# Float64 weights to float32 by an integer sum on POOL, one softmax form for all batches, one-sum pooling, and a reordered beginning

## The chip, the cores and the metric

One core of one Trainium2 chip runs the whole program. The metric is the device time of one launch in microseconds (us); the kernel before takes 567.24 us, the median of 3 runs (565.05 to 570.59). Engines: PE is TensorE, DVE VectorE, ACT ScalarE, POOL GpSimd, SP the engine that issues most DMAs.

## The reference

Attention over keys and values pooled by 8, then a mixing block:

```python
B, H, S, D = 8, 8, 576, 64;  Sp = 72;  d_model = H * D = 512
k_p = k.reshape(B, H, Sp, 8, D).mean(axis=3)
v_p = v.reshape(B, H, Sp, 8, D).mean(axis=3)
scores = scale * np.matmul(q, k_p.transpose(0, 1, 3, 2))
attn = softmax(scores)                       # sum + 1e-9 below the line
x = np.matmul(attn, v_p)                     # -> (B, S, 512)
theta = x @ w_theta
zr, zi = x * np.cos(theta), x * np.sin(theta)
y = einsum('ts,bsd->btd', w_tok_r, zr) + einsum('ts,bsd->btd', w_tok_i, zi)
u = x + y
return u + np.maximum(u @ w_ch, 0.0)
```

`q`, `k`, `v` are float32. The four weights (`w_theta` and `w_ch` 512 x 512, `w_tok_r` and `w_tok_i` 576 x 576) arrive as float64, and the kernel reads them as pairs of 32-bit words.

## The kernel before, in words

Work is cut into small generators ("streams"), and a long table of words, `SCHEDULE`, says which generator takes its next step; a last letter v, g or a gives that step's free choice of engine to DVE, POOL or ACT. So the table sets the order of instructions on every engine, and each engine works in that order. The word before the dot names the kind and batch: `k`, `v`, `Q` load (Q also transposes), `K` and `V` pool, `S` is a softmax tile of 128 queries, `X` attention times V, `T` the rotation by theta, `Z` and `M` split and mix over tokens, `F` the last channel matmul. `h` is a 128-row piece of `w_theta`, `c` one of `w_ch`, `w` a piece of the token weights, `W` its transposes into `WTh` and `WTl`. `D` is a warm-up of 12 matmuls.

A float64 becomes float32 in `to_f32` (line 342). The high words, read as float32 and scaled, give a value t that after a shift by 3 and the sign bit holds the truncated float32 (line 373). The low words, scaled by a power of two (362), are multiplied by the power of two of t (masked out at line 375, product at 382 or, for `w_ch`, at 378), which makes a second float32 number s. The weight is t + s. For `w_theta` an identity matmul pair sums them in PSUM (409, 410); for `w_ch` a tensor add does (397); for the token weights each 128 x 128 block is transposed on PE (455), and a second matmul adds the transposed s (458). Each weight is then kept as a high part (rounded to fp32r) and a low part.

Softmax (`soften`, line 699) has two forms. For batches 0 and 1 (`SUMS_ON_ACT` = 2) ACT takes each of the 8 heads alone: an exponential out of PSUM with the negative maximum as bias and the sum as a second output (771), plus a scaling of the maxima (767) and the epsilon (775). From batch 2 on DVE subtracts the maxima for all heads (779), ACT takes one exponential of 576 columns (783), and DVE sums (785); the epsilon is a 73rd column of `e_eps`. The second and fourth tile of batch 0 keep theirs in `spare`.

Pooling over 8 rows (`pool_sum`, 497) is three adds that halve the width; batch 0's keys and values are pooled on PE instead (575, 577). POOL's tensor operations of 512 or more columns are cut in two (`InHalves`).

Of the kernel before, what the change touches and what calls it, by code (L numbers as in the profile page):

```python
# [30 lines left out]
k0.0 k0.2 w0.0 w0.0g K0.0 k0.1 K0.0v K0.2 K0.2a h0 h0a K0.1 Q0.0 Q0.0 Q0.2 w0.0a K0.1a h0a w0.0v K0 Q0.2 h1 w0.0 h0v  # L31
K0a K0 h0 K0a Q0.0v h0 Q0.1 Q0.3 h1a h0v h1v S0.0 h0 h1g w0.1 S0.0 Q0.2v S0.0 Q0.1 Q0.1v h1 Q0.3 S0.1 h1 Q0.3v S0.1
S0.2 h2 h0v S0.0 S0.0 v0.2 S0.1 w0.1v D h0 S0.1 S0.2 w0.1a Q0.4 S0.2 h1g S0.0g h2v S0.0g h1 h2v Q0.4 h1a w0.1v w0.1
S0.1 Q0.4a k1.0 h3 v0.1 S0.1g w0.1 v0.0 w1.0 S0.3 h2a S0.3 S0.0 w1.1 w2.0 S0.4 h1 h2 h3v S0.3 S0.1v h2 h3a Q1.1 V0.2
V0.1 h2v K1.0v w0.0 S0.0a h3a S0.3 S0.1 h3 w0.0v h2 S0.0 S0.0v S0.3 h3 V0.0 h3v k1.1 S0.2 S0.1v w1.1v w0.1g w1.0a
w1.1a S0.4 h3 S0.1 h2a V0v S0.3g S0.2 S0.2g S0.2v w3.0 S0.1a V0 S0.3g w2.1 S0.4 Q1.0 w1.0a w1.1a w1.0v K1.1g W0 h2
w1.0 X0.0.1 h3a X0.0.1v k1.2 S0.4 X0.0.3 h3 W0v w1.1 w1.0 S0.2 w1.1 v1.0 S0.2a X0.0.2 X0.0.0 w2.0a X0.0.2a X0.0.3a
S0.3 X0.0.0a Q1.1 S0.3a Q1.0 T0.1g w1.0v Q1.1a w1.1v S0.2 S0.3 W1 S0.4 Q1.2 W0 K1 T0.0a S0.3v S0.4g w2.0a S0.2v w2.0a
T0.0v V1.0v S0.4v T0.0 w3.0a Q1.0a Q1.3 w2.0 K1a W0 w3.0a w3.1 W1a T0.1v T0.0 S0.4 w2.1a w3.0v S0.4a S0.4 W0a w2.0
w2.0g w3.0 w4.0 T0.1 w2.1a S0.4v W1 X0.2.1 w2.1a T0.1 W1 K1.2g T0.0 T0.0 w3.0 T0.0 W0 w2.1 w3.1a T0.0a X0.2.1v W1v W1  # L40
# [95 lines left out]
F7.2.1v F7.2.1 F7.0.1v F7.0.1a F7.0.1  # L136
"""

EARLY, EXACT, V_ON_PE, K_ON_PE, Q_ON_PE, SUMS_ON_ACT = 2, 1, 1, 1, 2, 2
BY_ROWS = 1


@with_exitstack
def tile_attn_moe(
    ctx: ExitStack,
# [198 lines left out]
    def to_f32(raw, t, sign, power, s):  # L347
        words = raw.rearrange("p (n w) -> p n w", w=2)
        lo, hi = words[:, :, 0], words[:, :, 1]
        ti, pi = t.bitcast(I32), power.bitcast(I32)  # L350

# [910 lines left out]
```

## Time and profile before

| What | us |
|---|---|
| Median of 3 runs | 567.24 |
| Lowest, highest | 565.05, 570.59 |
| Span of the profiled execution, first to last instruction | 562.9 |
| PE, DVE, ACT, POOL busy in that span | 546.2, 460.1, 338.6, 354.9 |

The profile is one execution. No device time of that execution is listed beside its span, so it is set against the median of the runs. Rows of the timeline give start and duration; PE's matmuls are pipelined, so the distance of two starts tells their price better than the duration does.

### The profile page before, as it was taken

The page shows a single profiled execution, that of the slowest core. Times are in us where ns is not written, and L with a number is a line of the kernel's source. Part 1 is how long each engine was busy: PE and PEld are TensorE (multiplying, and loading weights), DVE is VectorE, ACT ScalarE, POOL GpSimd, SP SyncE. Part 2 cuts the span into 40 slices and gives each one's busy share as a digit, 9 for nine tenths or more (in the row PEclk, how much of TensorE's full clock was granted, in tenths as well). Part 3 has the DMA queues.
Part 4 walks back from the last instruction along what each step waited for, and adds up shares of the span by engine and source line. Part 5 has one row for each costly group of instructions (what it writes and reads, how often), then busy time and mean ns, then how long its engine had stood idle before and what let it go on. Part 6 is the DMA issues. An engine that isn't in the chain of part 4 may idle for free.

```text
span 562.9 us, 11666 instructions
## 1 busy us (share of the span) xinstructions
PE 546.2 (97%) x4084; PEld 515.3 (92%) x4084; DVE 460.1 (82%) x888; ACT 338.6 (60%) x774; POOL 354.9 (63%) x504
## 2 busy tenths in 40 slices
PE   6999989999999999999999999999999999999997
PEld 5777779989999999998999999999999999999996
DVE  5989999889989898799988888988858788577355
ACT  3789899798875785657824578558215575233010
POOL 4455766499477988687969786765825564271330
PEclk9989999999999999999999999999999999999999
DMA  8998121574577686365487575437326330321017
GB/s 253 268 298 196 48 82 62 110 137 106 112 130 108 121 144 118 65 136 109 67 149 136 93 117 108 71 64 127 49 45 107 59 57 0 55 36 22 1 22 127
DMA packets 231802, 57.85 MB, mean 103 GB/s; under 512 B 218688, under 2 KB 220352, under 8 KB 231744
## 3 DMA queue, kind: packets, MB, share of 16 engines
q1 hardware_dynamic: 226768, 56.47, 51.0%
q10 hardware_dynamic: 4976, 0.64, 0.8%
q8 instruction: 32, 0.52, 0.4%
q14 instruction: 26, 0.21, 0.2%
HBM read 37.81 MB, written 9.44 MB: 84 GB/s over the span
## 4 chain that ended last, share of the span: by engine, by line
PE 78%; ACT 5%; DVE 5%; DMA 4%; SPq 3%; issue 2%; POOL 1%; ACTq 1%; DVEq 0%; POOLq 0%
PE py L1058 33%; PE pt L970 15%; PE pf L1091 13%; PE pv L923 7%; PE s L728 4%; PE px L984 2%; SPq L878 2%; DMA early<-in_v_dram 2%; DMA WTh_st<-in_moe_w_theta_dram 1%; PE vpp L575 1%; PE wt L455 1%; ACTq L1133 1%; DMA out_dram<-rz 1%; POOL eraw L191 1%; PE pe L824 1%
## 5 line engine op out<-in xcount | busy, mean ns | idle before, releaser
L1058 PE MATMUL py<-WTl,zh 128*128 128x288 f32 x576 | 82.5, 288 | 0.0
L1058 PE MATMUL py<-WTh,zh 128*128 128x288 f32 x576 | 81.2, 288 | 1.3 <-ACT zh L206 1.2
L1058 PE MATMUL py<-WTh,zl 128*128 128x288 f32 x576 | 81.1, 288 | 0.0
L1058 PEld LDWEIGHTS py<-WTh,zh 128*128 128x128 f32 x576 | 74.3, 189 | 1.9 <-ACT zh L206 1.4
L1058 PEld LDWEIGHTS py<-WTl,zh 128*128 128x128 f32 x576 | 74.9, 189 | 0.3
L1058 PEld LDWEIGHTS py<-WTh,zl 128*128 128x128 f32 x576 | 74.6, 189 | 0.4 <-POOL zl L191 0.2
L191 POOL TENSOR_TENSOR zl<-z,zh 128x256 fp32r<-128x256 f32 (+2 forms) x64 | 52.0, 844 | 28.0 <-ACT zh L206 15.3
L1068 DVE TENSOR_TENSOR xT<-py,xT 128x288 f32<-128x288 f32 x64 | 28.2, 448 | 29.3 <-PE py L1058 29.1
L976 ACT ACTIVATE g<-pt,c_magic 128x512 f32<-128x512 f32 x35 | 23.9, 684 | 40.8 <-PE pt L970 29.1
L1091 PE MATMUL pf<-uh,chh 128*128 128x288 f32 x256 | 43.9, 294 | 0.1
L191 POOL TENSOR_TENSOR ul<-xT,uh 128x288 fp32r<-128x288 f32 x40 | 32.9, 838 | 17.3 <-ACT uh L206 13.6
L1091 PE MATMUL pf<-uh,chl 128*128 128x288 f32 x256 | 41.8, 286 | 0.0
L1091 PE MATMUL pf<-ul,chh 128*128 128x288 f32 x256 | 41.8, 286 | 0.0
L970 PE MATMUL pt<-th,xh 128*128 128x512 f32 x148 | 39.5, 389 | 0.1
L191 POOL TENSOR_TENSOR xl<-xT,xh 128x256 fp32r<-128x256 f32 x42 | 32.1, 787 | 11.4 <-ACT xh L206 7.5
L970 PE MATMUL pt<-th,xl 128*128 128x512 f32 x148 | 38.0, 379 | 0.0
L970 PE MATMUL pt<-tl,xh 128*128 128x512 f32 x148 | 38.0, 379 | 0.0
L783 ACT ACTIVATE e_eps<-e_eps 128x576 f32<-128x576 f32 (+1 forms) x30 | 20.5, 685 | 28.4 <-DVE e_eps L779 28.2
L728 PE MATMUL s<-kpT,qT 128*128 128x144 f32 x256 | 36.5, 287 | 0.8 <-DVE qT L208 0.3
L1091 PEld LDWEIGHTS pf<-uh,chh 128*128 128x128 f32 x256 | 36.1, 189 | 1.0 <-ACT kpT L206 0.3
L1098 DVE SCALAR_TENSOR_TENSOR xT<-pf,xT 128x288 f32<-128x288 f32 x64 | 27.5, 442 | 10.2 <-PE pf L1091 9.8
L206 ACT CAST zh<-z 128x1152 fp32r<-128x1152 f32 (+1 forms) x19 | 20.6, 1092 | 24.9 <-PE py L1058 19.9
(267 smaller groups left out, 1471.1 us busy)
## 6 DMA issues: line engine op xcount, KB each, us to landing
out_dram<-R SPq DMA_DIRECT2D x112, 72.0 KB, 2.1
kpst<-in_k_dram SPq DMA_DIRECT2D x15, 512.0 KB, 4.3
vpst<-in_v_dram SPq DMA_DIRECT2D x28, 256.0 KB, 4.0
qsst<-in_q_dram SPq DMA_DIRECT2D x96, 72.0 KB, 3.1
eraw<-G SPq DMA_DIRECT2D x96, 60.0 KB, 2.2
eraw<-G SPq DMA_DIRECT2D x96, 40.0 KB, 2.0
WTh_st<-in_moe_w_theta_dram SPq DMA_DIRECT2D x4, 512.0 KB, 8.1
wcraw<-in_moe_w_ch_dram SPq DMA_DIRECT2D x4, 512.0 KB, 3.3
```

Source lines behind the costliest of these rows:

```text
L191: nc.gpsimd.tensor_tensor(out[:, r], a[:, r], b[:, r], op)
L206: nc.scalar.copy(out, src)
L728: nc.tensor.matmul(scs[c // 2][:n, 2 * SP * (c % 2) : 2 * SP * (c % 2 + 1)], qT[:, c, t0 : t0 + n], kpT[:, c, :], start=True, stop=True,)
L783: nc.scalar.activation(e[:n], e[:n], AF.Exp, scale=scale)
L878: nc.sync.dma_start(blocks(Ex, jj, i), blocks(Gx, i, jj))
L923: nc.tensor.matmul(as_written(pv[:, :gn]) if pair else pv[:, :gn], l, by_turns(r) if pair else r, start=i == 0, stop=i == len(terms) - 1,)
L970: nc.tensor.matmul(as_written(pt), l[:, c, :], by_turns(r[:, c, :]), start=i == 0, stop=i == 11)
L976: nc.scalar.activation(halves(g), in_order(pt), AF.Identity, bias=c_magic)
L1058: nc.tensor.matmul(as_written(py[:, :n]), l[:, kk, :], by_turns(r[:, kk, t]), start=i == 0, stop=i == 3 * NK - 1,)
L1068: nc.vector.tensor_tensor(halves(u), in_order(py[:, :n]), halves(u), ALU.add)
L1091: nc.tensor.matmul(as_written(pv[:, :n]), l[:, kk, o], by_turns(uhl[r][:, kk, t]), start=i == 0, stop=i == 11,)
L1098: nc.vector.scalar_tensor_tensor(halves(oT), in_order(pv[:, :n]), 0.0, halves(oT), ALU.max, ALU.add)
```

## The change

The weights' two parts are now added as integers. The low words, scaled by 2^-29, become an integer `low` (the last three bits, rounded), and POOL adds it to the integer t in one uncut instruction of 512 or 576 columns. So t is the finished float32; masks, products, the second number, and the matmuls that summed the two parts go, and `identr` with them. Batches 0 and 1 take the other batches' form of softmax (`SUMS_ON_ACT` = 0); `spare` gets an epsilon column. Where DVE pools (and not in fine steps), it does so in one reduction over a strided view. The first 577 words of the schedule become 556 in another order and with other letters; the 1,495 behind them are the same.

```diff
 SCHEDULE = """
-k0.0 k0.2 w0.0 w0.0g K0.0 k0.1 K0.0v K0.2 K0.2a h0 h0a K0.1 Q0.0 Q0.0 Q0.2 w0.0a K0.1a h0a w0.0v K0 Q0.2 h1 w0.0 h0v
...
-EARLY, EXACT, V_ON_PE, K_ON_PE, Q_ON_PE, SUMS_ON_ACT = 2, 1, 1, 1, 2, 2
+EARLY, EXACT, V_ON_PE, K_ON_PE, Q_ON_PE, SUMS_ON_ACT = 2, 1, 1, 1, 2, 0
...
-    identr = const([P, P], F32R, "identr")
-    nc.vector.tensor_copy(identr, ident)
...
+    spare_at = {"e": (0, 584), "en": (584, 1160), "g": (1160, 1672), "sn": (1672, 2184)}
+    nc.gpsimd.memset(spare[:, 0:584], 1e-9)
...
             nc.scalar.activation(t, hi.bitcast(F32), AF.Copy, scale=2.0**-112)
...
-        if s is not power:
-            if pick() == "a":
-                nc.scalar.activation(s, lo.bitcast(U32), AF.Copy, scale=2.0**-52)
...
+        if pick() == "a":
+            nc.scalar.activation(low, lo.bitcast(U32), AF.Copy, scale=2.0**-29)
+        else:
+            ENG[pick()].tensor_scalar(low, lo.bitcast(U32), 2.0**-29, None, ALU.mult)
+        yield
...
         nc.vector.scalar_tensor_tensor(ti, ti, 3, sign, ALU.logical_shift_left, ALU.bitwise_or)
         yield
-        nc.vector.tensor_scalar(pi, ti, -0x800000, None, ALU.bitwise_and)
-        yield
-        if s is power:
-            nc.vector.scalar_tensor_tensor(
-                s, lo.bitcast(U32), 2.0**-52, power, ALU.mult, ALU.mult
-            )
-        else:
-            ENG[pick()].tensor_tensor(s, f32(s), power, ALU.mult)
-        yield
+        nc.gpsimd.tensor_tensor(ti, ti, low, ALU.add)
+        yield
...
-            ENG[pick()].tensor_tensor(t, t, s, ALU.add)
-            yield
...
-        sum_ = bank([P, DM], bank_of(c))
-        nc.tensor.matmul(sum_, ident, t, start=True, stop=False)
-        nc.tensor.matmul(sum_, identr, s, start=False, stop=True)
-        yield
...
-            nc.tensor.matmul(
-                out, t[rows, cols], ident[rows, rows], is_transpose=True, start=True, stop=False
-            )
-            nc.tensor.matmul(out, s[rows, cols], identr[rows, rows], start=False, stop=True)
+            nc.tensor.transpose(out, wts[m][0][rows, cols], ident[rows, rows])
...
+        if e == "v" and not fine:
+            by_pool = "p (r d) -> p d r" if len(t.shape) == 2 else "p c (r d) -> p c d r"
+            nc.vector.tensor_reduce(dst, t.rearrange(by_pool, d=D), AX.X, ALU.add)
+            return
...
-            nc.vector.tensor_reduce(sm[:n], e_eps[:n], AX.X, ALU.add)
+            nc.vector.tensor_reduce(sm[:n], e_all[:n], AX.X, ALU.add)
```

Three places show what the new table does. The first is SP's queue of loads up to V of batch 0 (`early<-in_v_dram`; `WTh_st` stages `w_theta`, `wraw` the token weights, `qsst` and `qst` hold queries, `kpst` keys). Before, from its eighth load on:

```order
L387 DMA WTh_st<-in_moe_w_theta_dram 128x1024
L629 DMA qsst_0_162<-in_q_dram 128x8x64
L629 DMA early<-in_q_dram 128x8x64
L440 DMA wraw_1_211<-in_moe_w_tok_i_dram 128x128
L441 DMA wraw_1_211<-in_moe_w_tok_i_dram 128x1024
L387 DMA WTh_st<-in_moe_w_theta_dram 128x1024
L533 DMA vprst_260<-in_v_dram 64x1x512
L629 DMA qst_291<-in_q_dram 64x8x64
L519 DMA kpst_0_317<-in_k_dram 128x2x512
L387 DMA WTh_st<-in_moe_w_theta_dram 128x1024
L522 DMA early<-in_v_dram 64x2x512 x4
```

Now, from the sixth load on:

```order
L603 DMA qsst_0_151<-in_q_dram 128x8x64
L603 DMA early<-in_q_dram 128x8x64
L603 DMA qsst_0_151<-in_q_dram 128x8x64
L603 DMA qst_191<-in_q_dram 64x8x64
L507 DMA vprst_219<-in_v_dram 64x1x512
L374 DMA WTh_st<-in_moe_w_theta_dram 128x1024
L603 DMA early<-in_q_dram 128x8x64
L414 DMA wraw_1_247<-in_moe_w_tok_i_dram 128x128
L415 DMA wraw_1_247<-in_moe_w_tok_i_dram 128x1024
L496 DMA early<-in_v_dram 64x2x512 x2
L374 DMA WTh_st<-in_moe_w_theta_dram 128x1024 x2
L496 DMA early<-in_v_dram 64x2x512 x2
```

The first half of V moved ahead of two `w_theta` pieces and of the next batch's keys. Of the first loads, which are not shown, the three of keys now stand together at the head, ahead of one piece of `w_theta` and one of `w_tok_r`.

The second place is PE around the first transposed weights (`vpp` pools V, `ths` sums a piece of `w_theta`, `pe` and `per` transpose attention, `wt` the token weights, `pv` is attention times V). Before:

```order
L575 MATMUL vpp_371<-early,ident 128x128 x8
L824 MATMUL pe_1_405<-ident,spare 128x128 x4
L409 MATMUL ths_412<-WTh_st,ident 128x512
L410 MATMUL ths_412<-WTl_st,identr 128x512
L832 MATMUL per_0_415<-ident,en_0_297 64x128
L575 MATMUL vpp_371<-early,ident 128x128 x8
L409 MATMUL ths_449<-WTh_st,ident 128x512
L410 MATMUL ths_449<-WTl_st,identr 128x512
L832 MATMUL per_1_452<-ident,spare 64x128
L455 MATMUL wt_0_483<-ident,wsrc_a 128x128
L458 MATMUL wt_0_483<-identr,wsrc_b 128x128
```

Now:

```order
L549 MATMUL vpp_232<-early,ident 128x128 x8
L807 MATMUL per_0_345<-ident,en_0_278 64x128
L428 MATMUL wt_0_357<-ident,wsrc_a 128x128 x8
L549 MATMUL vpp_232<-early,ident 128x128 x8
L799 MATMUL pe_1_384<-ident,spare 128x128 x4
L807 MATMUL per_1_416<-ident,spare 64x128
L799 MATMUL pe_2_418<-ident,en_2_381 128x128 x4
L898 MATMUL pv_0_0_428<-eh_0_300,Ve 128x256
```

The sums are gone, a transposed block is one instruction, and the first eight blocks stand ahead of the second half of V.

The third place is POOL behind its memsets (`wsrc_a` and `wsrc_b` are t and s of the token weights, `en` and `spare` normalised attention, `WTl_st` the low part of `w_theta`). Before:

```order
L195 TENSOR_SCALAR wsrc_a<-wraw_0_121 128x288 x2
L195 TENSOR_SCALAR chl_st<-WTh_st 128x256 x2
L191 TENSOR_TENSOR WTl_st<-WTl_st,eraw_114 128x256 x2
L191 TENSOR_TENSOR en_0_297<-e_eps,ri_0_258 128x256 x2
L191 TENSOR_TENSOR en_0_297<-e_eps,ri_0_258 128x64
L191 TENSOR_TENSOR spare<-spare,ri_1_314 128x256 x2
L191 TENSOR_TENSOR wsrc_b<-wsrc_b,eraw_114 128x288 x2
L191 TENSOR_TENSOR spare<-spare,ri_3_418 128x256 x2
```

Now:

```order
L369 TENSOR_TENSOR WTh_st<-WTh_st,WTl_st 128x512
L369 TENSOR_TENSOR wsrc_a<-wsrc_a,wsrc_b 128x576
L190 TENSOR_TENSOR en_0_278<-e_eps,ri_0_244 128x256 x2
L190 TENSOR_TENSOR en_0_278<-e_eps,ri_0_244 128x64
L369 TENSOR_TENSOR WTh_st<-WTh_st,WTl_st 128x512
L369 TENSOR_TENSOR wsrc_a<-wsrc_a,wsrc_b 128x576
L190 TENSOR_TENSOR spare<-spare,ri_1_316 128x256 x2
L190 TENSOR_TENSOR spare<-spare,ri_1_316 128x64
L190 TENSOR_TENSOR en_2_381<-e_eps,ri_2_349 128x256 x2
```

Every weight piece now passes POOL, and its adds alternate with the normalisations.

## Rows read from the trace of the kernel before

**Rows 1.** The page's busy line: us, share of the span, instructions.

```profile
PE 546.2 (97%) x4084; PEld 515.3 (92%) x4084; DVE 460.1 (82%) x888; ACT 338.6 (60%) x774; POOL 354.9 (63%) x504
```

**Rows 2.** Busy time by stretch: length, PE, PEld, DVE, ACT, POOL, granted clock, DMA share, GB/s.

```profile
0.00:73.00 73.00, 65.79 (x428) 53.44 (x428) 62.72 (x122) 57.87 (x168) 38.78 (x56) 0.98 0.77 205
73.00:80.00 7.00, 4.44 (x36) 3.67 (x35) 6.97 (x14) 5.83 (x13) 5.02 (x7) 1.00 0.28 95
80.00:144.00 64.00, 62.70 (x488) 59.69 (x487) 57.63 (x118) 54.24 (x182) 47.74 (x71) 1.00 0.49 107
144.00:563.00 419.00, 413.25 (x3140) 398.46 (x3138) 332.83 (x638) 220.62 (x414) 263.39 (x373) 1.00 0.49 85
```

**Rows 3.** Who PE waited for, to 200 us: total, times, longest.

```profile
PE kpp L575 <- DMA kpst<-in_k_dram: 4.7, 1, 4.7
PE py L1058 <- ACT zh L206: 1.2, 1, 1.2
PE vpp L575 <- DMA early<-in_v_dram: 1.2, 1, 1.2
```

**Rows 4.** PE's timeline from 28 us: start, duration, what, count, idle before.

```profile
28.56 3.64 PE L575 MATMUL vpp<-early,ident 128*128 128x128 f32 x16 [1.17 <-DMA early<-in_v_dram]
...
32.48 1.02 PE L409 MATMUL ths<-WTh_st,ident 128*128 128x512 f32 x2
...
33.57 0.27 PE L832 MATMUL per<-ident,en 128*64 128x128 f32 x1
33.67 1.95 PE L575 MATMUL vpp<-early,ident 128*128 128x128 f32 x16
```

**Rows 5.** Busy time by stretch around the late V piece; columns as in rows 2.

```profile
0.00:28.00 28.00, 21.43 (x171) 18.57 (x171) 21.31 (x45) 16.61 (x59) 12.50 (x22) 1.00 0.97 260
28.00:32.00 4.00, 3.44 (x16) 3.47 (x17) 3.29 (x7) 3.97 (x27) 0.00 (x0) 0.57 1.04 255
```

**Rows 6.** PE's timeline around eight transposed blocks of token weights.

```profile
60.28 0.27 PE L455 MATMUL wt<-ident,wsrc_a 128*128 128x128 f32 x1
...
61.83 0.62 PE L984 MATMUL px<-ident,xT 128*128 128x128 f32 x4
62.29 0.60 PE L636 MATMUL pq<-ident,qsst 128*128 128x128 f32 x4
```

**Rows 7.** DVE's busy time in line 375 to 150 us (count), clock, DMA.

```profile
0.00:150.00 150.00, 9.50 (x17) 0.99 0.61 152
```

**Rows 8.** The same for line 378.

```profile
0.00:150.00 150.00, 3.03 (x4) 0.99 0.61 152
```

**Rows 9.** The same for line 382.

```profile
0.00:150.00 150.00, 6.15 (x8) 0.99 0.61 152
```

**Rows 10.** The same for line 397.

```profile
0.00:150.00 150.00, 2.08 (x3) 0.99 0.61 152
```

**Rows 11.** Groups to 150 us, the later softmax form: out<-in, shapes, count, busy us, mean ns.

```profile
L779 DVE TENSOR_TENSOR e_eps<-s,mx 128x576 f32<-128x576 f32 x3 | 2.3, 758 | 0.2
L785 DVE TENSOR_REDUCE sm<-e_eps 128x8 f32<-128x584 f32 x3 | 2.2, 744 | 0.9 <-ACT e_eps L783 0.9
L783 ACT ACTIVATE e_eps<-e_eps 128x576 f32<-128x576 f32 x3 | 2.1, 686 | 0.1
```

**Rows 12.** ACT's busy time in line 771 to 150 us (count), clock, DMA.

```profile
0.00:150.00 150.00, 26.50 (x161) 0.99 0.61 152
```

**Rows 13.** Groups on POOL to 150 us: a one-input cast, a two-input product.

```profile
L208 POOL CAST xh<-xT 128x512 fp32r<-128x512 f32 x5 | 3.5, 709 | 8.9 <-DVE xT L934 5.5 <-ACT xT L932 3.4
L191 POOL TENSOR_TENSOR wsrc_b<-wsrc_b,wpow 128x288 fp32r<-128x288 f32 x6 | 5.5, 937 | 4.9 <-DVE wpow L375 4.9
```

**Rows 14.** DVE's timeline: one product alone, the next beside a POOL instruction.

```profile
44.00 0.74 DVE L382 TENSOR_TENSOR wsrc_b<-wsrc_b,wpow 128x576 fp32r<-128x576 f32 x1
44.67 1.16 DVE L382 TENSOR_TENSOR wsrc_b<-wsrc_b,eraw 128x576 fp32r<-128x576 f32 x1
```

**Rows 15.** POOL's timeline at the same moment.

```profile
44.12 1.10 POOL L208 CAST xh<-xT 128x512 fp32r<-128x512 f32 x1 [0.73 <-ACT xT L932]
```

More of the change, by code (lines that the diff above doesn't have):

```diff
@@ L36 @@
[L36 to L40, printed above, removed]
@@ L325, in tile_attn_moe @@
     eraw0 = work([P, 5 * 3 * P], F32, "eraw", "eraw0")
-    powers = [work([P, S], F32, "R", "wpow", bufs=2), eraw0[:, NC * 320 : NC * 320 + S]]
+    powers = work([P, S], I32, "R", "wpow", bufs=2)
     early = work([P, NK, DM], F32, "z", "early").rearrange("p a b -> p (a b)")
@@ L341, in temp, with to_f32 @@
         return work([P, width], F32, tag, f"{tag}{b}_{m}")
-    def to_f32(raw, t, sign, power, s):
+    def to_f32(raw, t, sign, low):
         words = raw.rearrange("p (n w) -> p n w", w=2)
         lo, hi = words[:, :, 0], words[:, :, 1]
-        ti, pi = t.bitcast(I32), power.bitcast(I32)
+        ti = t.bitcast(I32)
         if pick() == "a":
@@ L389, in channel_weights @@
         tmp = tmp_of(c)
-        if bank_of is None:
-            t, s = tmp[:, 0:DM], tmp[:, DM : 2 * DM]
-            sign = powers[0][:, 0:DM].bitcast(I32)
-            if c == 0:
-                nc.gpsimd.memset(sign, 0)
-            yield from to_f32(raw, t, sign, s, s)
-            ENG[pick()].tensor_tensor(t, t, s, ALU.add)
-            yield
-            hi, lo = held_of()
+        t, low, sign = tmp
+        yield from to_f32(raw, t, sign, low)
+        hi, lo = held_of()
+        if scale is None:
             copy(pick(), hi[:, c, :], t)
@@ L444, in token_weights @@
             wa = work([P, 4 * S], F32, "uh", "wsrc_a")
-            wb = work([P, 4 * S], F32R, "ul", "wsrc_b")
+            wb = work([P, 4 * S], I32, "ul", "wsrc_b")
             wbufs["t"] = [wa[:, 0 : 2 * S], wa[:, 2 * S :]]
@@ L449, in token_weights @@
         t, s = (x[:, cols] for x in wts[m])
-        yield from to_f32(raw, t, signs[part], powers[part], s)
+        yield from to_f32(raw, t, signs[part], s)
     def turn_weights(m):
         def turned(out, rows, cols):
-            t, s = wts[m]
-            nc.tensor.matmul(
-                out, t[rows, cols], ident[rows, rows], is_transpose=True, start=True, stop=False
-            )
-            nc.tensor.matmul(out, s[rows, cols], identr[rows, rows], start=False, stop=True)
+            nc.tensor.transpose(out, wts[m][0][rows, cols], ident[rows, rows])
         o = slice(P * m, P * m + (P if m < 4 else 64))
@@ L1188, in tile_attn_moe @@
                     stage("WTh", I32)[:, DM * (8 + c % 2) : DM * (9 + c % 2)].bitcast(F32),
-                    stage("WTl", F32R)[:, DM * c : DM * c + DM],
+                    stage("WTl", I32)[:, DM * c : DM * c + DM],
+                    signs[c % 2][:, 0:DM],
                 ),
-                lambda c: f"ths{c}",
             ),
@@ L1199, in tile_attn_moe, with channel_words @@
     A(1)
+    def channel_words(c):
+        t = work([P, 2 * POOL * D], F32, "kv", f"wcts{c}")
+        sign = powers[:, 0:DM]
+        if c == 0:
+            nc.gpsimd.memset(sign, 0)
+        return t[:, 0:DM], t[:, DM : 2 * DM].bitcast(I32), sign
     for c in range(NC):
@@ L1205, in tile_attn_moe @@
                 lambda c: work([P, 2 * S], I32, "qs", f"wcraw{c}"),
-                lambda c: work([P, 2 * POOL * D], F32, "kv", f"wcts{c}"),
-                None,
+                channel_words,
             ),
```

224 lines of the change are left out of this document (112 added, 112 removed).

## The prediction

> **What bounds the kernel now.** I read the page's busy line first: TensorE (PE) is busy 97% of the span [rows 1]. That share is an average, so the next view is the busy time by stage [rows 2]. From 144 us to the end PE is busy 413.25 of 419 us; in the 64 us before that 62.70; in the first 80 us only 65.79 + 4.44 = 70.23. The first 80 us are also where VectorE (DVE) is nearly as full, 62.72 + 6.97 = 69.7 us, with ScalarE (ACT) at 63.7; in the last stage DVE has 332.83 of 419. So PE sets the time everywhere, and in the first 80 us DVE stands close behind it. The reordered part of the schedule ends near 144 us; behind it every engine but DVE's pooling keeps its order.
>
> PE's waits [rows 3] come next. There are few: 4.7 us until the first keys land, 1.2 us for a piece of V, 1.2 us for the first `zh`. Around the second one the timeline [rows 4] shows more than a wait: the 16 matmuls of a V piece that start at 28.56 take 3.64 us, the same 16 at 33.67 take 1.95. The granted clock explains it [rows 5]: 0.57 in 28 to 32 us, a mean of the 1.2 and 2.4 GHz levels, after light 64-wide matmuls and the wait; 1.00 before. So the late V piece cost 1.2 us of wait and about 1.6 us of half clock.
>
> **What comes off PE.** Two groups of matmuls go.
>
> The channel sums: an identity matmul of the high part (two records) and one of the low part, four times. From the first record at 32.48 to the next operation at 33.57 is 1.09 us [rows 4]; 4 x 1.09 = 4.4 us.
>
> The token-weight transposes: 41 blocks, each a transpose plus an accumulating matmul of the low part; the second goes. Eight pairs run from 60.28 to 61.83 [rows 6], 0.194 us a pair. What is left is a plain transpose, and four of those run from 61.83 to 62.29, 0.115 each. 41 x 0.079 = 3.2 us.
>
> Together 7.6 us. PE is busy nearly without a gap around these, so they lie on the path if the other engines don't take PE's place. The warm-up (12 matmuls) moves from behind the third score tile to behind the keys' transposes, where PE would wait for copies anyway; I cost it at nothing and keep its own 24 x 0.11 = 2.7 us (at the same 0.115) as a bound on both sides.
>
> **What DVE, ACT and POOL gain and lose.** DVE loses the exponent masks, line 375: 9.50 us in 17 [rows 7]; the scaled products of lines 378 and 382: 3.03 and 6.15 us [rows 8, 9]; the sums of line 397: 2.08 us [rows 10]. That is 20.8 us. It gains the softmax of ten tiles in the form that later batches have: a subtraction (0.758 us for a full tile, half of it for a half) and a sum (0.744) [rows 11]: 10 x (0.76 + 0.74) = 15.0 us. Net -5.8 us. The letters of the schedule also hand copies of `qT`, `kpT`, `er` and `WTh` to ACT; I count about 4 us more off DVE before 80 us, an estimate from the forms' durations. Against that the one-sum pooling is not in the trace. By elements at the sum's price (1024 against 584) it is 1.3 us; three adds today are about as much; at twice that, ten of them cost 13 us over 144 us. I take no change, by the nearest row.
>
> ACT loses the exponentials head by head: 26.50 us for ten tiles [rows 12], replaced by 10 x 0.686 = 6.9 us [rows 11]. That pays for all it takes over. One tile's softmax also gets shorter: eight heads at 2.65 us become a subtraction, one exponential and a sum, 2.2 us.
>
> POOL gains 17 integer adds (nine of 576 columns, eight of 512) that no row shows. From below, a one-input cast of 512 takes 0.709 us; from above, two stretched halves of 288 at the mean of 0.937 are 1.9 us [rows 13]. I take 1.6, nearer the two-input row: 17 x 1.6 = 27 us, 12 to 32 at the ends. It loses ten products, two sums and four scalings, some 15 us. In 0 to 144 us it has 38.78 + 5.02 + 47.74 = 91.5 us busy [rows 2], so there is room. The new add is the last step of every weight: behind it on POOL stand the normalised `en` tiles, for which PE waits, and `xl`.
>
> DVE and POOL stretch each other: with a POOL cast of 1.10 us running [rows 15], the same DVE product took 1.16 instead of 0.74 us [rows 14], 0.42 us lost. If one in three of the new adds does that, it is 17 / 3 x 0.42 = 2.4 us of DVE, inside the nearly 10 us it gains.
>
> The rule that speaks against this change is in the Trainium skill, "SBUF — State Buffer", section "SBUF: two separate sides": DVE and GpSimd share a port pair as an exclusive lock, and the loser waits for the whole instruction of the other. Before, POOL's two-input work was cut in halves; the new adds are not. By that rule an add can hold up a DVE instruction for its full length, which is the slow rival below; the rows of the stretched pair show a loss of 0.42 us beside an instruction of 1.10, less than a full block.
>
> **The order of the loads.** Ahead of the first V piece SP now issues 4,608 KB where it issued 6,144, by the shapes of the transfers. At the 260 GB/s of the first 28 us [rows 5] those 1.5 MB are 5 to 6 us. V's first half then stands before PE asks for it, so the 1.2 us wait and the 1.6 us at half clock should go: 2.8 us. The keys are now the first three loads (1,152 KB instead of 1,728 with a weight piece between them), so pooling of keys ends about 2 us sooner; the queries land later behind 512 KB of channel weights, so the first scores start about 1 us later. I put zero for the start.
>
> **The sum.** Off PE 7.6; V's wait and slow matmuls 2.8; of the waits behind the last weights and the first `zh` (7 - 4.44 = 2.6 us in 73 to 80 [rows 2], the 1.2 of rows 3 among them) half, since DVE is ahead there, 1.3. Against it new waits: the first transposed weights now stand on PE ahead of V's second half and need DVE, ACT and then a POOL add, about 1.3 us; and 1.4 us for stretched DVE steps that reach PE. Net 7.6 + 2.8 + 1.3 - 2.7 = 9.0 us. The profiled span is 562.9 us, no time of that execution beside it is given, and the median of the three runs is 567.24, so 4.3 us lie around the span. 562.9 - 9.0 + 4.3 = 558.2 us.
>
> **Rivals.**
>
> *The gain is spent early.* The head becomes bound by the chain of a weight (load, two conversions, sign, shift, add on an in-order POOL), not by PE. For it: DVE and ACT were at 87% and 80% of the first 80 us, and a new order meets new waits. Against it: both lose work. If the 2.8 and 1.3 us are not won and 5 us of waits come in, 7.6 - 5.0 = 2.6 us are left: 564.6 us, within 1%.
>
> *The lead is lost behind 144 us.* The rest runs at the pace of something else, POOL's and the transposing DMAs' chains. For it: no engine's order changes there. Against it: PE is idle for 5.75 us in 419. Half the gain lost: 562.7 us, also within 1%.
>
> *Slower: POOL's uncut adds block DVE.* Place: the first 80 us, with 13 of the adds. If each blocks DVE for its whole 1.6 us, DVE loses 20.8 us against 9.8 us of relief, 11 us more than now. Its idle time is 80 - 69.7 = 10.3 us, most of it before the first scores; if 3 us of it can be used, `zh` comes 8 us later than today: 575 us. It decides from about 0.75 us of blocking per add (9.8 / 13). The rows show 0.42 in a stretched case, and most instructions are not stretched.
>
> *The matmuls taken out were hidden.* If PE only waited for DVE in the first 80 us, taking matmuls out gives nothing. Then the gain is DVE's 9.8 us less the 2.4: 7.4 us, nearly the same time, 559.8. It doesn't change the sign.
>
> **How the numbers follow.** Forecast with its near twin: 0.76. Gain spent early 0.13, lead lost 0.06, blocked DVE 0.05. About 1% is what a measurement of this kernel can tell from no change; 1% faster is 561.6 us. The forecast's own spread is the warm-up's 2.7 us and the unknown waits, 553.5 to 563, so a little of it (0.03) is within 1%, and a little of the second rival is faster. Faster 0.74, same 0.20, slower 0.06. The range reaches from all waits won (7.6 + 2.8 + 2.6 and some of the warm-up, 553.5) to the first rival's 564.6, rounded to 565.
>
> **What would show it right or wrong.** Right: the PE records of the channel sums and the second matmul of a transposed block are gone; plain blocks start 0.115 us apart; the first `py` matmul, at 79.3 us before, starts near 70; the V matmuls of 16 run in about 2 us with no wait before them; DVE's busy time in the first 80 us falls. Wrong: PE shows waits over 1 us for POOL's adds or for `en`; an add of 576 takes over 2 us; a new slice with a low granted clock; or PE's idle time grows behind the reordered part.

## The result, and the profile after

The changed kernel takes 571.73 us (median of 7 runs, 569.14 to 575.74) beside 565.34 for the kernel before (7 runs, 563.35 to 570.59). The ratio is 1.0100, with a 95% interval of 1.0067 to 1.0133: slower by one per cent, where 558.2 us and a gain of 1.6% had been forecast, and above the range's end of 565.0. (Ratios and intervals here are those of undisturbed runs, and they are not quotients of the medians.) The profiled execution took 572.32 us, with a span of 570.5.

What the change was to remove from TensorE did go. The page's busy line answers to [rows 1], and the eight blocks of transposed weights to [rows 6]:

```profile
PE 544.3 (95%) x4031; PEld 513.3 (90%) x4031; DVE 458.9 (80%) x834; ACT 324.8 (57%) x619; POOL 360.7 (63%) x507
...
59.33 1.04 PE L428 MATMUL wt<-ident,wsrc_a 128*128 128x128 f32 x8
```

Eight plain blocks now take 1.04 us with the last one's 0.27 of latency, 0.11 us apart, and no record of a channel sum is left. The busy time by stage shows where the time went instead (columns as in [rows 2]):

```profile
0.00:73.00 73.00, 61.59 (x382) 50.18 (x382) 55.72 (x97) 52.73 (x99) 41.52 (x52) 0.98 0.82 212
73.00:80.00 7.00, 6.24 (x49) 5.76 (x49) 6.38 (x13) 6.85 (x13) 6.78 (x10) 1.00 0.07 19
80.00:144.00 64.00, 57.55 (x413) 53.47 (x412) 56.69 (x87) 41.30 (x91) 44.13 (x67) 0.95 0.41 92
144.00:570.00 426.00, 418.87 (x3190) 403.87 (x3189) 340.13 (x639) 223.88 (x420) 268.28 (x381) 1.00 0.49 85
```

In 80 to 144 us PE was busy 62.70 us before and is busy 57.55 now, at a clock of 0.95. Behind 144 us it has 418.87 - 413.25 = 5.6 us more to do than before and idles 7.1 us where it idled 5.75. So most of the loss comes about ahead of 144 us, in 80 to 144 above all, and the rest of the program hands it on. PE's waits up to 145 us, answering to [rows 3] (they sum to 18.5 us in 18 waits, 11.0 in 13 before):

```profile
PE kpp L551 <- DMA kprst<-in_k_dram: 3.6, 1, 3.6
PE px L959 <- DVE er L821: 3.5, 1, 3.5
PE vpp L549 <- DMA early<-in_v_dram: 1.9, 1, 1.9
PE pv L898 <- DVE xT L909: 1.3, 1, 1.3
```

The new one is the second. PE's timeline around it (start, us, engine, line, tiles, shapes, count, [idle before <- releaser]):

```profile
112.82 1.35 PE L1033 MATMUL py<-WTh,zl 128*128 128x288 f32 x9
117.66 1.09 PE L959 MATMUL px<-ident,xT 128*128 128x128 f32 x4 [3.49 <-DVE er L821]
118.40 2.06 PE L945 MATMUL pt<-th,xh 128*128 128x512 f32 x4
120.25 1.92 PE L945 MATMUL pt<-tl,xh 128*128 128x512 f32 x4
121.95 1.91 PE L945 MATMUL pt<-th,xl 128*128 128x512 f32 x4
123.66 0.33 PE L807 MATMUL per<-ident,en 128*64 128x128 f32 x1
```

The wait costs 3.49 us. From the first of the twelve `pt` matmuls behind it to the next record it is 5.26 us (118.40 to 123.66), 2.6 us too long (2.70 in a run below): the granted clock of 116.9 to 123.8 us is 0.51, the lower level. DVE, for which PE waits, and what POOL does at that time:

```profile
110.75 0.20 DVE L762 RECIPROCAL ri<-sm 128x8 f32<-128x8 f32 x1
111.06 4.33 DVE L778 TENSOR_TENSOR en<-e_eps,ri 128x64 f32<-128x64 f32 x1
115.31 0.74 DVE L737 TENSOR_REDUCE mx<-s 64x8 f32<-64x576 f32 x1
...
111.00 0.41 POOL L207 CAST uh<-xT 128x288 fp32r<-128x288 f32 x1
111.39 1.18 POOL L190 TENSOR_TENSOR en<-e_eps,ri 128x256 f32<-128x256 f32 x2
112.54 1.40 POOL L190 TENSOR_TENSOR xl<-xT,xh 128x256 fp32r<-128x256 f32 x2
113.91 2.19 POOL L190 TENSOR_TENSOR kpst<-kpst 128x256 f32<-128x256 f32 x3
```

A product of 64 columns, 0.2 us by itself, takes 4.33 us on DVE; such a row, many times its usual length beside POOL's work, is called a hold below. Through all of it POOL runs one instruction behind another without a gap; the second of the three `kpst` adds ends at 115.30, the third depends on it and starts at about 115.4, and there DVE's product ends (115.39). None of these is one of the new integer adds. In the old order this tile's two products, 128x512 and 128x64, both stood on DVE (the second, at 112.43 beside POOL's `kpst` adds, took 0.78 us); the new order gives the first to POOL.

The forecast's other place, V [rows 4, 5], is not repaired; it is now the second half that comes late: 1.94 us of wait, and 3.62 us for the 16 matmuls that take 1.95 at full clock.

```profile
31.67 3.62 PE L549 MATMUL vpp<-early,ident 128*128 128x128 f32 x16 [1.94 <-DMA early<-in_v_dram]
```

The two operations that no row of before showed (groups up to 144 us): the one sum, and the integer add by size.

```profile
L472 DVE TENSOR_REDUCE vp<-vpst 128x128 f32<-128x1024 f32 x4 | 7.9, 1987 | 0.0
L472 DVE TENSOR_REDUCE kp<-kpst 128x128 f32<-128x1024 f32 x3 | 5.8, 1931 | 1.1 <-DMA kpst<-in_k_dram 1.1
L369 POOL TENSOR_TENSOR wsrc_a<-wsrc_a,wsrc_b 128x576 int32<-128x576 int32 x9 | 14.4, 1595 | 12.7 <-DVE wsrc_a L367 12.7
L369 POOL TENSOR_TENSOR WTh_st<-WTh_st,WTl_st 128x512 int32<-128x512 int32 x4 | 5.7, 1435 | 14.2 <-DVE WTh_st L367 14.2
L369 POOL TENSOR_TENSOR wcts<-wcts 128x512 int32<-128x512 int32 x4 | 5.1, 1271 | 3.2 <-DVE wcts L367 3.1
```

The 17 adds take 14.4 + 5.7 + 5.1 = 25.2 us, 1.48 each (forecast 1.6). The one sum takes 1.93 to 1.99 us, where 1.3 was the estimate and three adds took 0.69 + 0.42 + 0.29 = 1.4 before.

### The profile page after: what moved, and what is told of

It reads as the page before. It is cut to its first block, busy times and chain, and to the rows that moved or that the text cites. A ratio compares the mean times of both kernels' runs of the same rounds, so it can differ in the third digit from the quotient of the medians.

```text
span 570.5 us, 11343 instructions
## 1 busy us (share of the span) xinstructions
PE 544.3 (95%) x4031; PEld 513.3 (90%) x4031; DVE 458.9 (80%) x834; ACT 324.8 (57%) x619; POOL 360.7 (63%) x507
## 4 chain that ended last, share of the span: by engine, by line
PE 64%; DVE 16%; DMA 5%; ACT 5%; SPq 4%; issue 3%; POOL 1%; ACTq 0%; DVEq 0%; POOLq 0%
PE py L1033 28%; PE pf L1066 12%; PE pt L945 12%; PE pv L898 4%; PE s L702 3%; SPq L853 3%; DMA early<-in_v_dram 2%; PE px L959 2%; PE kpp L549 1%; DVE wsrc_a L367 1%; DVE vp L472 1%; DMA early<-in_q_dram 1%; DMA eraw<-G 1%; DVE sm L760 1%; DVE en L778 1%
## 5 line engine op out<-in xcount | busy, mean ns | idle before, releaser
L190 POOL TENSOR_TENSOR zl<-z,zh 128x256 fp32r<-128x256 f32 (+2 forms) x76 | 60.2, 823 | 27.4 <-ACT zh L205 14.6
L190 POOL TENSOR_TENSOR ul<-xT,uh 128x288 fp32r<-128x288 f32 x42 | 34.4, 835 | 17.8 <-ACT uh L205 13.6
L758 ACT ACTIVATE e_eps<-e_eps 128x576 f32<-128x576 f32 (+1 forms) x38 | 26.0, 684 | 33.3 <-DVE e_eps L754 33.0
L1066 PEld LDWEIGHTS pf<-uh,chl 128*128 128x128 f32 x256 | 35.7, 189 | 0.0
```

The costliest lines, as they stand in the source:

```text
L190: nc.gpsimd.tensor_tensor(out[:, r], a[:, r], b[:, r], op)
L758: nc.scalar.activation(e[:n], e[:n], AF.Exp, scale=scale)
L1066: nc.tensor.matmul(as_written(pv[:, :n]), l[:, kk, o], by_turns(uhl[r][:, kk, t]), start=i == 0, stop=i == 11,)
```

## The experiments

Times are given as ratios to the kernel before, run on the same chip in between (medians 566.3 to 567.3 us), with 95% intervals. Theory A: one DVE instruction held up by POOL makes the loss. B: DVE is full, so the time only moves. C: the one sum. D: the edits gain and the order loses. E: the edits themselves lose.

**The product on Pool: one letter of the order.**

```
- ... M0.1.1a S1.3v S1.3 ...
+ ... M0.1.1a S1.3g S1.3 ...
```

> One letter of the changed kernel's order: the 128x64 product of S1.3 (4.33 us on VectorE at 111.06, where the same operation alone takes 0.18) goes to Pool, behind the 128x512 product of the same tile. Theory A (one VectorE instruction held up by Pool's uninterrupted work makes most of the loss: 3.5 us of TensorE wait at 117.66, and 2.7 us more for 12 matmuls at the lower clock behind it): about 565.5 us against 571.7, the row of 4.33 us gone, no half clock at 117 to 124. Theory B (VectorE is full through the whole head, so the time only moves to its next late result): above 569.5, another wait of 2 us or more between 111 and 140. Theory C (sums in one instruction and poolings moved to VectorE make the loss): above 569.5 here, and the gain is in the run without them.

Measured: 1.0006 (0.9970 to 1.0043). From 1.0100 that is 0.94%, 5.3 us, and the two intervals do not touch. In its trace the same stretch of DVE, then of PE:

```profile
110.49 0.20 DVE L762 RECIPROCAL ri<-sm 128x8 f32<-128x8 f32 x1
110.61 0.70 DVE L737 TENSOR_REDUCE mx<-s 64x8 f32<-64x576 f32 x1
...
114.11 0.63 PE L959 MATMUL px<-ident,xT 128*128 128x128 f32 x4 [0.20 <-DVE er L821]
114.74 1.13 PE L945 MATMUL pt<-th,xh 128*128 128x512 f32 x4
115.71 1.03 PE L945 MATMUL pt<-tl,xh 128*128 128x512 f32 x4
116.57 1.03 PE L945 MATMUL pt<-th,xl 128*128 128x512 f32 x4
117.44 0.27 PE L807 MATMUL per<-ident,en 128*64 128x128 f32 x1
```

The wait falls from 3.49 to 0.20 us and the twelve matmuls from 5.26 to 2.70. A holds, B does not: one letter takes back the whole difference to before. The same trace has a hold once more, in the part whose order the change left alone, and there PE does not wait for it:

```profile
249.74 4.23 DVE L778 TENSOR_TENSOR en<-e_eps,ri 128x64 f32<-128x64 f32 x1
...
249.92 1.35 PE L1033 MATMUL py<-WTh,zl 128*128 128x288 f32 x9
251.11 1.27 PE L1033 MATMUL py<-WTl,zh 128*128 128x288 f32 x9
252.21 1.27 PE L1033 MATMUL py<-WTh,zl 128*128 128x288 f32 x9
253.31 1.27 PE L1033 MATMUL py<-WTh,zh 128*128 128x288 f32 x9
```

PE has 36 matmuls in its queue that need nothing from DVE. The hold is 4.2 us here too; what it costs is decided by what PE has in front of it. The kernel before has this row as well (shown below).

**Three adds again.** The branch with `tensor_reduce` in `pool_sum` is taken out.

```
-        if e == "v" and not fine:
-            by_pool = ...
-            nc.vector.tensor_reduce(dst, t.rearrange(by_pool, d=D), AX.X, ALU.add)
-            return
```

> The changed kernel with VectorE's poolings as three adds again (1.14 + 0.29 us in the trace of before, against 1.91 to 2.0 for the one sum); all else, the order too, as changed. Theory C (the one sum costs): 10 sums ahead of 144 us, 0.5 us each, 5 us off VectorE's queue there, so about 567 us. Theory A: the blocked product at 111 stays, the gain is at most what a shorter queue ahead of it gives, above 570.

Measured: 1.0147 (1.0107 to 1.0186), not a gain of 5 us but nominally a loss of 2.6. C falls. One pooling of its trace, against one of the changed kernel, shows what the three adds meet:

```profile
130.31 1.58 DVE L471 TENSOR_TENSOR vpst<-vpst 128x512 f32<-128x512 f32 x2
131.93 2.54 DVE L476 TENSOR_TENSOR vp<-vpst 128x128 f32<-128x128 f32 x1
...
61.41 2.00 DVE L472 TENSOR_REDUCE vp<-vpst 128x128 f32<-128x1024 f32 x1
```

Adds of two SBUF operands are held up by POOL, here for 4.1 us in all; the sum with one operand took 1.9 to 2.0 us wherever it stood.

**The old order with all edits**, and **the old order with the conversion alone.** In the first the table of before is used, with the steps that no longer exist taken out; in the second the softmax and the poolings are as before too.

```
- w0.0 w0.0g w0.0a w0.0v w0.0 w0.0 w0.0v
+ w0.0 w0.0g w0.0a w0.0v w0.0 w0.0
```

> All edits of the change (integer conversion, softmax of batches 0 and 1 on VectorE's sums, one-sum pooling), in the order of before; the conversion's steps stand where before had them, the integer add in place of the product. Theory D (the edits gain what was forecast off TensorE, 7.6 us at most, and the new order of the first 560 pieces throws it away): 558 to 562 us. Theory E (the edits themselves cost, Pool's integer adds of 1.3 to 1.9 us and the one sums above all, and the order was made for them): 568 or more. Theories A and C lie between: A says that the product at 111 is not blocked in this order (it stands on VectorE behind the 128x512 one), so below 566.

> The integer conversion alone in the order of before: sums of batches 0 and 1 on ScalarE and poolings by three adds as before. What it takes from TensorE is 4.4 us (channel sums) and 3.2 us (blocks turned once). Theory D: 558 to 561, within 2 us of the run with all edits, or below it if the one sum costs. Theory E with Pool's integer adds as the cause: 567 or more here too. If the matmuls taken out were hidden anyway: 565, as before.

Measured: 1.0202 (1.0167 to 1.0236) and 1.0078 (1.0048 to 1.0108). Both are slower than before; D falls in the form in which it stood, the edits gain nothing by themselves. E's times (568 and 567 or more) are met; that POOL's adds are the cause is argued, not shown. In the first, tile S0.2's subtraction stands ahead of the last reads of S0.0 in the buffer that both use, so some exponentials are other ones: the new softmax does not fit the old order as it stands. In the second, PE's waits to 145 us begin thus:

```profile
PE kpp L545 <- DMA kpst<-in_k_dram: 4.8, 1, 4.8
PE wt L428 <- POOL wsrc_a L369: 2.4, 2, 1.2
PE wt L428 <- ACT e_eps L742: 1.8, 1, 1.8
PE s L698 <- DVE qT L583: 1.6, 1, 1.6
```

The integer add (line 369) is now what the first transposed weights wait for, as the forecast feared for the new order, where it is 0.8 us.

**V earlier**, on top of the product on Pool.

```
- v0.0 Q0.3a S0.1 h2 ... h3 ... S0.2 v0.1 S0.3
+ v0.0 v0.1 Q0.3a S0.1 h2 ... h3 ... S0.2 S0.3
```

> The kernel with the product on Pool, and the load of V's second half of batch 0 issued right behind the first half, ahead of the last two pieces of w_theta (it stood behind them). Theory F (V's lateness is the next loss: TensorE waits 3.0 us at 32.09 and then runs 3.4 us at the lower clock, 1.7 us lost): 4 to 5 us less than the run with the product on Pool, 562 to 563. Theory G (the queues of VectorE and ScalarE behind set the pace, so that time gained ahead of 40 us is waited away again before 144): within 1.5 us of it, 566, with the wait at 32 gone and others of its size grown.

Measured: 1.0038 (1.0010 to 1.0067), no gain. V's 16 matmuls start at 28.94 instead of 32.09 and take 1.95 us, and what follows them starts at 30.73, 3.6 us ahead. Then PE waits 1.31 us for ScalarE's copy of V and 0.62 for DVE's masked product, and the granted clock falls for 10 us:

```profile
37.00:47.00 10.00, 10.00 (x33) 5.84 (x32) 7.78 (x12) 6.83 (x16) 4.38 (x7) 0.50 1.07 311
```

At 47 us it is 1.2 us behind. That is what theory G said.

**Those copies earlier too**, and the pooling that waits for a late load behind the two shifts: `V0a V0` directly behind `V0.1`, `K1.0v k1.1` behind `h2`.

> The run with V earlier, where what TensorE then waited for ahead of 47 us is drawn forward too: ScalarE's copies of V and VectorE's masked product stand right behind V's last pooling on TensorE, and the pooling of batch 1's first K piece, for whose load VectorE waited 2.2 us, behind the two integer shifts of w_theta. Theory F' (the gain from V was lost to 1.9 us of waits for these and 5 us of low clock that followed): about 561 to 563. Theory G: within 1.5 us of the run with the product on Pool, 566 to 568.

Measured: 1.0098 (1.0065 to 1.0130), worse. PE's waits to 145 us sum to 13.8 us, less than the 15.7 of the run with the product on Pool, but PE waits 0.94 and 1.03 us at 32 to 35 us, and the lower clock now lasts 13.7 us:

```profile
34.70:48.40 13.70, 13.28 (x36) 7.18 (x37) 10.63 (x16) 7.93 (x18) 6.42 (x9) 0.50 0.81 213
```

**Work in the wait for V.** On top of the product and the two further moves below, 24 dead matmuls behind the weights' first blocks.

```
+    p = bank([P, 512], "warm_again")
+    for _ in range(24):
+        nc.tensor.matmul(p[:, 0:P], ident, ident, start=True, stop=True)
```

> The run with the product on Pool and two more VectorE instructions moved, with 24 matmuls of dead work (128 columns each) on TensorE in its wait for V's second half, 2.6 us at 31. If the low clock behind that wait (3.4 us at 1.2 GHz, 1.7 us lost) comes from TensorE's standing still: it is gone, and the time 1 to 2 us less, about 564.5. If it is the DMA or what follows that sets the pace: no change, within 1 us; if the dead work delays the poolings of V, up to 1.5 us more.

Measured: 1.0022 (0.9989 to 1.0055). The clock stays at its upper level from 10 to 563 us (1.00 in that stretch): with the wait for V, the low clock behind it is gone. That standing still alone brings it about is not shown, and two rows speak against it: in this run PE waits 1.89 us for `Vr` at 103 us, and in the run with blocks turned twice (below) 2.65 us for V, and the clock stays up. The dead work started 1.1 us late, behind a copy on ScalarE, and took 5.6 us, twice the wait that it was to fill; V's matmuls came 4.5 us later, and 2.1 of that was left at 139 us. No gain.

**Integer adds in halves**, on top of the product on Pool.

```
-        nc.gpsimd.tensor_tensor(ti, ti, low, ALU.add)
+        ENG["g"].tensor_tensor(ti, ti, low, ALU.add)
```

> The kernel with the product on Pool, and the 17 integer adds cut in halves of 256 or 288 columns like Pool's other work. The forecast's rival (an uncut add of 1.3 to 1.9 us holds VectorE up for its length): the stretched rows at 45.0 (1.96 us) and 98.0 (2.23) shrink by half a microsecond to one each, 2 us less or more over the head. Theory A (it is uninterrupted runs of many Pool instructions that hold VectorE up, not the length of one): no change, within 1.5 us, the rows at 98.0 and 101.0 still above 2 us.

Measured: 1.0108 (1.0057 to 1.0160), a per cent worse, not better. The stretched row at 45 us did shrink, from 1.96 to 1.35 us, as the rival had said, but the row behind it grew from 0.45 to 1.05, so nothing was won there. And the new timing ran `chl` on DVE into a longer hold; DVE and POOL:

```profile
97.14 5.38 DVE L383 TENSOR_TENSOR chl<-wcts,chh 128x512 fp32r<-128x512 f32 x1 [0.47 <-POOL chh L207]
...
97.06 1.18 POOL L190 TENSOR_TENSOR Vr<-vrx,mask 96x256 fp32r<-96x256 f32 x2
98.20 1.45 POOL L190 TENSOR_TENSOR en<-e_eps,ri 128x256 f32<-128x256 f32 x3
99.61 3.49 POOL L190 TENSOR_TENSOR zl<-z,zh 128x384 fp32r<-128x384 f32 x4
```

5.38 us for 0.68 us of work, beside pieces of 256 columns, none an integer add. PE waited 3.9 us behind it and the clock was at 0.50 for 6.8 us. So such a hold does not need a long POOL instruction. Whether shorter adds would gain without this accident stays open.

**Pairs of instructions by themselves**, three probes. The first:

> It leaves the whole computation out and writes zeros. It runs one VectorE operation at a time, released by a first short Pool instruction, beside what Pool runs behind that: nothing, six adds of 256 columns with outputs of their own, six adds chained on one tile, six casts, two integer adds of 512 columns; each pair twice. The operations: the 128x64 product, a cast of 288 columns, an add of 288 columns from PSUM, the one sum of 128x1024, the three adds that it replaces, a contiguous row sum of 128x584. Theory A (Pool keeps what the two share until it has a gap): the product and the cast take 0.2 to 0.4 us alone and chained (a gap behind each add), and about 4 us beside the six adds of their own. The other view (VectorE waits for one Pool instruction at a time): never above 0.7 us more, 1.3 beside an integer add. Theory C' (the one sum is slower but is not held up): 1.9 to 2.0 us beside everything; the three adds 1.4 alone and 3 or more beside Pool.

Measured: a DVE instruction that met POOL waited for one POOL instruction: an 8-column product took 0.17 us alone, 0.67 beside adds of 256 columns, 0.33 beside casts, 1.21 beside integer adds, and what followed it directly ran undisturbed (the 128x64 product 0.21). The one sum took 1.86 to 1.90 us beside everything; the three adds 1.43 alone and 2.23 beside POOL's adds. "Until a gap", as theory A has it, is not seen here; theory C' holds.

> It leaves the whole computation out and writes zeros. One VectorE operation at a time (the 128x64 product, or a 128x512 difference of two SBUF tiles) beside an uninterrupted run of eight or nine Pool instructions of 256 columns: plain adds, products with a broadcast factor, differences into float32r, or the mix that stood at 111 us; released with the run's first instruction, or by one or two short ScalarE copies later, so inside an instruction. In the first probe a short VectorE operation in front took the wait, 0.67 us, one Pool instruction. One at a time: no row above 1.4 us. A run that is held to its end: 4 us or more in some rows, and which ones says what it hangs on, the kind of Pool's instruction or the moment of the release.

Measured: 0.22 to 0.73 us for the product, 0.69 to 1.20 for the wide difference, again one POOL instruction at most.

> It leaves the whole computation out and writes zeros. The neighbourhood of 111 us is set up by itself, instruction for instruction on VectorE and Pool (row sum, reciprocal, the 128x64 product, a row maximum; on Pool two half products of 64 partitions, a sum, a difference, a cast, the two broadcast products that wait for the same reciprocal, two differences, the three steps of a pooling): as it stood, with the product's output in a tile of its own, with Pool's products not waiting for the reciprocal, and without the instructions ahead of them; each three times. If what stands there on the two engines decides: a product of 3 us or more in some of the cases, and the case in which it is short names the condition. If a product never takes above 1.4 us: the hold needs more than these two engines, and stays open.

Measured: 0.22 to 0.33 us in all twelve. The neighbourhood of the two engines alone does not bring the hold back.

**The run of Pool's shortened, in the kernel.** `K2.1g` becomes `K2.1v` in the changed kernel.

> The changed kernel with the pooling that stood last in Pool's run at 111 us (K2.1, four instructions) on VectorE as one sum; the 128x64 product stays on VectorE beside the run. If the product is held until Pool's run breaks off: it ends where the differences xl end, about 2.9 us long instead of 4.33, unless the run goes on with other work, and then as much longer. If it is held for a number of instructions that only chance decides: any length, with no break of Pool's at its end. One look, no interval.

Measured, in a single execution of 572.52 us: the product took 5.61 us, and PE waited 4.75. POOL's timeline shows that its run had not become shorter; work that stood behind moved up:

```profile
110.50 5.61 DVE L778 TENSOR_TENSOR en<-e_eps,ri 128x64 f32<-128x64 f32 x1
...
112.00 1.41 POOL L190 TENSOR_TENSOR xl<-xT,xh 128x256 fp32r<-128x256 f32 x2
113.36 0.42 POOL L207 CAST uh<-xT 128x288 fp32r<-128x288 f32 x1
113.75 2.28 POOL L190 TENSOR_TENSOR ul<-xT,uh 128x288 fp32r<-128x288 f32 x3
```

The run ends at 116.03 and the product with it, at 116.11. The hold thus ends where POOL's run breaks off, here, at 111 us in the changed kernel and at 250 us. It is no rule: `chl` and `uh` at 98 to 104 us came through after two or three instructions, and `chl` in the run with halves after eight: its row ends at 102.52, inside the fourth `zl` (101.92 to 103.10), where POOL's run has no break. Why, stays open.

**Blocks turned twice**, on top of the product on Pool: `nc.tensor.transpose(...)` in `turned` stands there twice.

> The kernel with the product on Pool, and each of the 41 transposed blocks of w_tok turned twice on TensorE, the second turn being dead work of the same result. By the block's 0.109 us that is 4.5 us of TensorE time put back. Theory H (the matmuls that the change took out were hidden: in the head TensorE waits for other engines, 15.7 us against 11.0 before): less than 1.5 us more. Theory I (TensorE sets the pace between its waits, and what was taken out is a gain that other terms ate): 3 to 4.5 us more, 570 to 571.5.

Measured: 1.0043 (1.0006 to 1.0079), 0.37% or 2.1 us more for 4.5 us of matmuls, with overlapping intervals; PE's waits to 145 us fell from 15.7 to 14.1. The runs don't decide between H and I: the two profiled executions differ by 3.4 us (spans of 566.9 and 563.5), and the extra blocks ahead of V's second half changed the clock too. It is 1.00 from 24 to 41 us here, although PE waits 2.65 us for V, and V's 16 matmuls take 2.02 us; with the product on Pool it fell to 0.52 at 35.4 to 37. How much of such work is hidden stays open.

**The softmax back on ScalarE**, on top of the product on Pool: `SUMS_ON_ACT` is 2 again.

> The kernel with the product on Pool, and the softmax of batches 0 and 1 back on ScalarE (eight short exponentials with their sums per tile, as before), in the new order. If the softmax part of the change gains by itself (0.75 us more per tile on VectorE against 8 exponentials of 0.2 or more on ScalarE): 2 to 4 us slower than the run with the product on Pool. If VectorE, full up to 80 us, is what sets the head's pace: 2 us faster. The forecast took it as even: within 1.5 us.

Measured: 1.0299 (1.0259 to 1.0338), some 17 us slower than the run with the product on Pool. PE waits 3.1, 3.0 and 2.0 us for the exponentials. The edit that the forecast took as even is worth 2.9% in this order.

**The old conversion in the new order.**

> The new order, the softmax edit, the one sum and the product on Pool, but the float64 words converted as before: mask and product (on Pool, in the place of the integer add) and the second matmuls into the channel sums and the transposed blocks are back. If the integer conversion gains in the new order what the forecast gave it (7.6 us of TensorE, a half of it hidden by the run with blocks turned twice, and 17 masks of 0.4 us off VectorE): 4 to 10 us slower than the run with the product on Pool, 571 to 577. If it gains nothing in either order (in the old one it lost 4.4 us): within 2 us of it.

Measured: 1.0340 (1.0287 to 1.0393), some 19 us slower than with the integer conversion. (The mask of `w3.0` stands between mask and product of `w2.0` in a tile that both use, so some weights are other ones; the instructions are those of before.) Not all of it is the conversion's: `chl` is held here too (5.38 us at 114.90) and PE waits 3.9 us behind it, as in the run with halves, which was 1.0% slower than the one with the product on Pool. With the old order, old conversion to new costs 0.8%; with the new order it gains 3.3%, of which by that run about 1% is the hold (an estimate). Order and edits need each other; together, with the product on Pool, they come out even with the kernel before.

**Two more instructions off DVE, then `chl` behind what PE waits for.** On top of the product on Pool, `chl` of the last piece goes to POOL and the cast `uh` at 101 us to ScalarE; then `chl` is put behind POOL's masked product.

```
- c3g M0.0.1 c3v V1g ... S1.2g X1.0.0 ... M0.0.0v
+ c3g M0.0.1 V1g ... S1.2g c3g X1.0.0 ... M0.0.0a
```

> The kernel with the product on Pool, and two more VectorE instructions that stand beside Pool's long run at 97 to 104 taken from it: the remainder chl of the last piece of w_ch (2.23 us at 98.01 where 0.68 is usual) goes to Pool, the cast uh (2.48 at 101.01 where 0.3 is usual) to ScalarE. Theory A: TensorE's waits of 0.8 and 1.3 us for what stands behind them on VectorE (at 100.78 and 103.88) go, 2 us less than the run with the product on Pool, about 565. Theory G (gains ahead of 144 us are waited away again): within 1 us of it.

> The run with the product on Pool and two more VectorE instructions moved, in which TensorE then waited 2.1 us for the masked V product behind chl on Pool: chl now stands behind that product and behind the softmax's products on Pool. Theory A: that wait falls to the 0.4 us that it was, about 1.5 us less, 565 or a ratio of 0.996 to the kernel before. Theory G: within 1 us of 566.3.

Measured: 0.9993 (0.9965 to 1.0022) and 0.9969 (0.9927 to 1.0012). The first took the two waits away and made one of 2.1 us for the product `Vr` behind `chl`; in the second that is 0.4. The last kernel is 1.3% below the changed one and nominally 0.3% below the one before (medians of all runs 563.87 and 567.33 us), a difference that its interval does not settle.

## Why the prediction was wrong, step by step

The step that failed is the cost of POOL to DVE, "one in three of the new adds ... 0.42", 1.4 us reaching PE. It looked at the new adds and priced one encounter from one row [rows 14, 15]. That row does not show "less than a full block": the cast ends at 44.12 + 1.10 = 45.22, about half a microsecond behind the start of the stretched product, so 0.42 us can be all that was left of it. What happened was a hold of an ordinary product by ordinary POOL work, through six instructions, at a moment when PE had nothing else: 3.49 us of wait and 2.6 us of low clock. Taking it away gave 5.3 us. The trace of the kernel before has such a hold, at a place where PE had other work, so its size was there to be read:

```profile
249.87 4.23 DVE L803 TENSOR_TENSOR en<-e_eps,ri 128x64 f32<-128x64 f32 x1
```

The slow rival had the mechanism (POOL blocks DVE) and the wrong instruction and place: cutting the adds gained nothing. The Trainium skill, "SBUF — State Buffer", section "SBUF: two separate sides", says that the loser of the shared pair waits for the whole instruction of the other. The probes agree with it (0.67 us beside adds of 0.7); in the kernel the wait was six to eight instructions long, 4.23 to 5.61 us, and there the measurement decides.

With that repaired the kernel stands at 1.0006, not at the forecast's 0.984. Of the 2.6% between forecast and result the hold is 0.94; the larger part is a gain that did not come, so other terms failed too. In the run with the product on Pool PE is busy 5.8 us less than before (540.4 against 546.2), where the sum has 9.2 (7.6 off PE and 1.6 of slow matmuls); and it is idle 6.4 us more (23.1 against 16.7), where the sum has 0.2 (2.7 of new waits less 1.2 and 1.3). Term by term:

- Off PE, 7.6: the pieces were right (0.11 us a block). Whether they all lie on the path is not settled by the blocks turned twice.
- V's wait and slow matmuls, 2.8: not won. Before, PE waited for V's first half; the working took 1.5 MB from ahead of that. Now the wait is for the second half, which SP issues behind two more pieces of `w_theta`: by the transfers that it counts, 6,144 KB stand ahead of it where 6,656 stood, 0.5 MB less. Where the wait was won by hand, later waits and 10 to 14 us of low clock took it back.
- The waits at 73 to 80, 1.3: PE's idle time there fell from 2.56 to 0.76 us, as forecast or better; but the first `py` starts at 76.52, 2.8 us earlier, not 9.
- New waits, 2.7: in sum 7.5 us, 18.5 against 11.0 up to 145; 4.7 with the product on Pool. This is the term that was sized worst.
- DVE's relief, nearly 10: in the first 80 us it is 69.7 - 62.1 = 7.6 us, but all of it ahead of 40 us; from 40 to 80 DVE is busy 39.3 of 40. The one sum taken as no change costs 0.5 us more than undisturbed adds, and less than disturbed ones.
- POOL's adds, 1.6: measured 1.48.

Of the rivals, "the gain is spent early" comes nearest to the kernel with the product on Pool, and of the 2.6 us that it leaves nothing is seen. "The lead is lost behind 144 us" is a small part at most: PE's idle time there grew by 1.4 us. "The matmuls taken out were hidden" stays open, and its bet on DVE was not paid.

## What to carry to other kernels

A short two-operand instruction on VectorE beside a long unbroken run on Pool may last through many of its instructions: let the two halves of one tile's work stand on the same engine, and look in the trace for rows that are many times their usual length before pricing anything else. Whether such a row costs anything is read from TensorE's queue at that moment. An order tuned for one set of edits is not a cost to be added to theirs: try the edits in the old order and the old ones in the new, since here both were slower than the kernel before, by 0.8 and 3.4% (a part of the second is a hold).

## What the runs showed of the hardware

- One DVE instruction was held through six to eight POOL instructions: 4.33, 4.23 and 5.61 us for 0.2 us of work, to the break of POOL's run, and 5.38 us for 0.68, with the run going on. Three probes with the two engines alone showed one instruction at most (0.67 and 1.21 us). What else it takes is open.
- A strided sum of 1024 elements to 128 takes 1.86 to 2.0 us, against 0.76 for a contiguous one of 584; by elements that would be 1.33. POOL did not lengthen it in the probe's ten cases (1.86 to 1.90 us).
- The lower clock was seen for 3.4 us behind one wait of 1.94 us, and for 10 and 13.7 us where that wait was replaced by two of 0.6 to 1.3 us. It was gone when TensorE did dead work in that wait, and also behind a wait of 2.65 us with eight more dead blocks ahead of it. So the length of the wait alone does not decide; what does is open.
